# A two-stage attention and feed-forward kernel on one Trainium2 core: the fourth layer by seven products for every group of weights, with one planner for the whole second stage

## The chip, the cores and the metric

The kernel runs on one core of a Trainium2 chip, in one launch. The metric is the device time of that launch in microseconds (us). Its engines are named as the profile names them: PE is the matrix engine and PEld its weight loads, DVE the vector engine, ACT the scalar engine, POOL the GpSimd engine, SP the engine that issues the transfers.

## The reference

Attention over chunks of 64 tokens (4 batches, 8 heads, 576 tokens, 64 per head), then two feed-forward parts over 2304 tokens, all in float32:

```python
x = softmax(scale * q_c @ k_c.T) @ v_c        # per chunk of 64, then 2304 x 512
x = ((x @ w_a) * (x @ w_b)) @ w_out           # 512 -> 1536 -> 512
h = x @ w_in                                  # 512 -> 2048
g = np.maximum(h, 0.0) + alpha * np.minimum(h, 0.0)
out = g @ w2_out                              # 2048 -> 512
```

## The kernel before

**Numbers.** Every operand of a matmul is split in two: a high part, which ACT writes by a copy to the matmul's own type (*high*), and the rest, which DVE or POOL subtracts (*low*). A product is three matmuls: low by high, high by low, high by high. The weights arrive as 64-bit words and are turned into float32 on the way.

**Tokens.** The 2304 tokens are five blocks: block 0 has 256 of them, blocks 1 to 4 have 512 each.

**First stage** (up to 488 us). Attention, then the first feed-forward part: its 1536 inner columns are 12 chunks of 128 in six groups of two. For each group and block there are the products `pa` and `pb` and the sums `po` (lines 463 and 549). Beside this, in small steps (`job`, line 381), the second part's weights are converted, split, added up and written to DRAM (`w2_...`).

**Second stage.** The 2048 inner columns are eight groups of two chunks, and the token blocks 1 to 4 are two pairs. So there are 16 units q: group q with blocks 1 and 2 for q = 0 to 7, group q - 8 with blocks 3 and 4 for q = 8 to 15. Block 0 goes along with the first eight.

- *Third layer* (`seven`, line 644, and `third_layer`, line 913). Two chunks by two blocks by two halves of the depth are a 2 x 2 product, done by seven products in place of eight (`sumX`, `sumY`, `sumZ`), with sums of weights S1 to S4 and sums of tokens T1 to T4. ACT keeps what is in a PSUM bank (`c<-sumX`), DVE adds to it (`c<-sumY`, `c<-sumZ`), then come the two slopes (`g`), on DVE or on ACT with a last step on DVE. Block 0 has a plain product of 256 columns (`ph`, "small").
- *Fourth layer, plain* (`plain_layer`, line 1108): six matmuls of 512 columns for each 128 tokens (`po4`, which the profile's lists shorten to po) and one addition of 128x512 to the output's accumulator `oacc`. This is used for q = 0 to 5, and for block 0 always.
- *Fourth layer by seven products* (`half_layer`, line 1217): for two units d and d + 1 together (d = 6, 8, 10, 12, 14): seven products, each in two steps (hf) of twelve matmuls of 256 columns (`l4X`, `l4Y`, `l4Z`), each step with one addition of 128x2x256. It needs sums of g over the units (`g_sum`, line 1185: four for each unit) and seven splits in high and low for each unit in place of four (`g_halves_of`, line 1199), and sums of the w2_out weights, which `outer` (line 1295) loads, subtracts, splits and writes back to DRAM for each group.

**Order.** The first stage and unit q = 0 (lines 1723 to 1750) stand in an order written out by hand. From q = 1 on a `Planner` (line 56) sets it: each task has its engines with a cost, the tasks that it waits for, a due time and the buffers that it needs. It walks a clock of its own and emits the task that could begin first. The costs set nothing but this order; each engine then works its queue in it, waiting for semaphores. PE has two lists of fixed order, third and fourth layer, which `merge` (line 827) deals out in turn.

**Buffers.** Four PSUM banks are for the third layer, four for the fourth. The weights of a unit (`from_dram`, line 428) have buffers of their own per pool and tag, those of the fourth layer (`o_slots`, line 877) four sets in turn. The rest of the second stage draws 2 KB tiles from one stock (`slot`, `give`). The tokens' sums for the first pair come from `t_ops` (line 597), for the second pair from `token_sums` (line 1361): sums on DVE or POOL, highs on ACT, lows on POOL in `t_ops`, on either in `token_sums`.

Of the kernel before, what the change touches and what calls it, by code (L numbers as in the profile page):

```python
# [9 lines left out]
F32 = mybir.dt.float32  # L10
# [34 lines left out]
class Task:  # L45
    def __init__(self, kinds, f, deps, due, slots, rounded):
        self.kinds, self.f, self.due, self.slots, self.rounded = kinds, f, due, slots, rounded
        self.deps = [d for d in deps if d is not None]
        self.users = []
        self.left = len(self.deps)  # L50
        self.end = None
        for d in self.deps:
            d.users.append(self)


class Planner:
# [23 lines left out]
    def run(self):  # L80
# [12 lines left out]
        def begin(t, e):  # L93
            b = max([at[e]] + [d.end + self.HOP for d in t.deps])
# [15 lines left out]
        while count:  # L110
# [8 lines left out]
            for e, ts in lists.items():  # L119
                found = [(begin(t, e), t) for t in ts]  # L120
                found = [x for x in found if x[0] is not None]
                if e in ("DVE", "ACT", "POOL"):
                    kept = []
                    for b, t in found:
                        if len(t.kinds) > 1:
                            score = {}
                            for o in t.kinds:
# [3 lines left out]
                                score[o] = max(at[o], b if o == e else 0) + w + t.kinds[o][0] + t.kinds[o][2]  # L131
# [15 lines left out]
            at[e] = t.end - self.LAP[e] if e != "SP" else b + 0.06  # L147
# [22 lines left out]
def tile_attention_moe_moe2(ctx: ExitStack, tc: tile.TileContext, qkv, w_a, w_b, w_out, w2_in, alpha, w2_out, out):  # L170
# [14 lines left out]
    FIRST = 6  # L185
    RESERVE, NEAR, PEN, SLOPES = 6, 6.0, 0.6, 0.0
# [342 lines left out]

    def l2_mm(g, j, o):  # L530
# [63 lines left out]
    T = {}  # L594
    T_AT = {"B11": "xh1", "B21": "xl1", "T2": "xl2", "T1": "xh3", "T3": "xl3", "T4": "xh4", "B22": "xl4"}

    def t_ops(j1, j2, pause=()):
# [3 lines left out]
        t1, t2 = tt[:, 0:2], tt[:, 2:4]  # L601
        steps = []
# [41 lines left out]
    def seven(i, q, j1, j2, bare=None):  # L644
# [12 lines left out]
        wh, wl = W2[q, w]  # L657
# [73 lines left out]
    def rest_of_second_stage(G_all):  # L731
# [30 lines left out]
        for tag, own in (("a", 3), ("gh", 4), ("gl", 4)):  # L762
            for i in range(6):
                pool, n = (gp, own) if taken[tag] % 6 < own else (spares[0], 6 - own)
                taken[tag] += 1
                k = rings[pool, tag] = (rings[pool, tag] + 1) % n
                if tag == "a":
                    free0.append((0.5 + i / 4, (pool, f"{tag}{k}")))
                else:
                    held.append((i // 2, (pool, f"{tag}{k}")))  # L770
# [15 lines left out]
        DMA = {"SP": (2.8, False, 0)}  # L786
# [17 lines left out]
        for q in range(1, 2 * n2):  # L804
# [7 lines left out]
        def length(x):  # L812
            return {"seven": 6 * PER512, "small": 12 * PER256, "plain": 6 * PER512, "half": 12 * PER256}[x[0]]
# [50 lines left out]
        W_USERS = {0: (("seven", 0), ("seven", 1), ("small", 0)), 1: (("seven", 5), ("small", 1)), 4: (("seven", 2), ("seven", 3)), 5: (("seven", 4), ("seven", 6))}  # L864
        front_task = {}

        def add_front(q):
            for i, k, tag in ((0, 0, "a"), (1, 1, "a"), (4, 0, "b"), (5, 1, "b")):
                before = [pe_task.get((n, q - 2, x)) for n, x in W_USERS[i]]
                front_task[q, i] = plan.add(DMA, lambda t, i=i, k=k, tag=tag: from_dram(q, i, k, tag), before)  # L870

        osets = [(0.0, 2), (0.0, 3)]
        TW = {}
        o_prev = [None]
        o_task = {}

        def o_slots(kind):
            def f(t):
                where = osets.pop(0)[1]
                w = wps[where]  # L880
                both = []
                for n in range(2):
                    x = w.tile([P, 512], F32R, tag="o" + "hl"[n], name="tw")
                    if kind[0] == "plain":
                        _, q, k = kind
                        nc.sync.dma_start(out=x.bitcast(F32), in_=dram[2 * q % M2, 2 + k, n])
                    else:
                        _, d, p = kind
                        _, i, half = PRODUCTS[p]
                        for k in range(2):  # L890
# [3 lines left out]
                            )  # L894
                    both.append(x)
                TW[kind] = where, both
            return f

        o_users = []

        def add_o(kind, deps=()):

            before = o_users[-4] if len(o_users) >= 4 else []
            t = plan.add(DMA, o_slots(kind), list(deps) + [o_prev[0]] + before)
            o_prev[0] = o_task[kind] = t
            o_users.append([])
            return o_users[-1]

        def done_with(kind):
            osets.append((plan.now, TW.pop(kind)[0]))  # L910


        def third_layer(q):
# [4 lines left out]
            def product(i, deps):  # L918
# [5 lines left out]
                def f(t):  # L924
                    if opens:
                        st[name] = open_bank(t, "sum" + name, [P, 512]), t.place
                    seven(i, q, j1, j2, st[name][0])

                w = front_task.get((q, A_AT[a][0]))
# [116 lines left out]
        def small(q, k, st, slopes):  # L1046
# [3 lines left out]
            def f(t):  # L1050
                ph = open_bank(t, "ph", [P, 256])
                run(ph, k_steps(W2[q, k], xh[0], xl[0]))
# [3 lines left out]
            t = plan.add(pe(12 * PER256), f, [front_task.get((q, k))], due["small", q, k])  # L1056
# [51 lines left out]
        def plain_layer(q, j, t0):  # L1108
# [4 lines left out]
            def f(t):  # L1113
                po = open_bank(t, "po4", [P, DM])
                steps = []
                for k in range(2):
                    wh, wl = W2[q, 2 + k] if q == 0 else TW["plain", q, k][1]
                    if j == 0 and q > 0:
                        gh, gl = (x[:, 256 * k + t0 * P:256 * k + t0 * P + P] for x in GZ[q])
                    else:  # L1120
                        gh, gl = (x[:, t0 * P:t0 * P + P] for x in (GH[q, k, j] if q else first_G[q, k, j]))
# [3 lines left out]
                if t0 == blocks[j][1] - 1:  # L1125
                    if q == 0:
                        n = {1: 0, 2: 1, 0: 2}[j]
                        for i, where in held:
                            if i == n:
# [666 lines left out]
```

## Time and profile before

| | us |
|---|---|
| runs of the kernel, median of 3 (lowest, highest) | 871.47 (870.28, 871.96) |
| the profiled execution, whole | 870.09 |
| its span, first to last instruction | 868.1 |
| PE busy in the span | 851.5 (98%) |
| DVE, ACT, POOL busy | 585.7 (67%), 398.2 (46%), 411.7 (47%) |
| DMA, mean rate | 182 GB/s |

The span is that of one execution under the profiler; about 2 us of the device time lie around it. Busy times of PE are of overlapping matmuls, so its rate is read from the starts of successive groups, not from the time of one matmul. Times of day in the text ("488.0") are us from the span's start.

### The profile page before, as it was taken

Reading aid. Unit: us, or ns where it says so; the run is one execution under the profiler, and the core shown is the slowest. Engines: PE = TensorE matmul, PEld = TensorE weight load, DVE = VectorE, ACT = ScalarE, POOL = GpSimd, SP = SyncE. Lnnn points to the kernel's source line nnn. Section 1 sums busy time; section 2 is a strip of 40 time slices with the busy share of each in tenths; the row PEclk is TensorE's granted clock in tenths of the full one; section 3 lists DMA queues with packets and bytes.
Section 4 is the critical chain, followed back from the end, with each engine's and each line's share of the span. In section 5 each row is a group of like instructions: output and inputs, shape, how many; then the busy total and the mean of one; then the engine's idle time right before and its main releaser. Section 6 shows DMA issues by size and latency. Waiting matters only on the chain.

```text
span 868.1 us, 14796 instructions
## 1 busy us (share of the span) xinstructions
PE 851.5 (98%) x5520; PEld 731.3 (84%) x5520; DVE 585.7 (67%) x886; ACT 398.2 (46%) x709; POOL 411.7 (47%) x337
## 2 busy tenths in 40 slices
PE   7999999999999999999999989999999999999997
PEld 6788788888888888888888868888888899999997
DVE  6983446766766767677672784666658975677877
ACT  4673544544453444444451424443435554454441
POOL 4552335345545544563461787353424574532441
PEclk9999999999999999999999999999999999999999
DMA  8853115447536744763590255667653788566335
GB/s 314 294 177 108 24 60 164 163 132 251 188 100 216 257 135 146 251 202 126 190 319 24 74 195 208 206 217 263 223 169 99 244 268 275 191 204 205 119 97 170
DMA packets 106230, 157.74 MB, mean 182 GB/s; under 512 B 11952, under 2 KB 59056, under 8 KB 106160
## 3 DMA queue, kind: packets, MB, share of 16 engines
q1 hardware_dynamic: 106160, 156.81, 55.6%
q8 instruction: 43, 0.70, 0.3%
q14 instruction: 27, 0.22, 0.1%
HBM read 114.30 MB, written 42.47 MB: 181 GB/s over the span
## 4 chain that ended last, share of the span: by engine, by line
PE 48%; POOL 5%; DVE 5%; issue 4%; ACT 1%; POOLq 0%; DVEq 0%
PE po L463 13%; PE sumX L663 10%; PE l4X L1238 6%; PE sumZ L663 5%; PE l4Z L1238 3%; POOL t L261 3%; PE pa L463 3%; PE pb L463 3%; PE sumY L663 2%; PE ph L463 2%; POOL gl L486 2%; PE l4Y L1238 2%; DVE t L251 1%; DVE t L248 1%; DVE wl L271 1%
## 5 line engine op out<-in xcount | busy, mean ns | idle before, releaser
L486 POOL TENSOR_TENSOR gl<-a_sb,gh 128x512 fp32r<-128x512 f32 (+1 forms) x60 | 77.3, 1289 | 134.1 <-ACT gh L481 133.5
L261 POOL TENSOR_TENSOR t<-t,raw 128x512 int32<-128x512 int32 x68 | 90.3, 1328 | 104.1 <-DVE t L251 82.8
L463 PE MATMUL po<-gh,wl 128*128 128x512 f32 (+1 forms) x240 | 89.1, 371 | 1.0 <-DVE xl L1641 0.8
L463 PE MATMUL pb<-xh,wl 128*128 128x512 f32 (+1 forms) x240 | 88.9, 370 | 0.2 <-POOL wl L271 0.2
L463 PE MATMUL pa<-xh,wl 128*128 128x512 f32 (+1 forms) x240 | 89.0, 371 | 0.0
L463 PE MATMUL po<-gl,wh 128*128 128x512 f32 (+1 forms) x240 | 88.4, 368 | 0.0
L463 PE MATMUL pa<-xl,wh 128*128 128x512 f32 (+1 forms) x240 | 88.4, 368 | 0.0
L463 PE MATMUL po<-gh,wh 128*128 128x512 f32 (+1 forms) x240 | 88.3, 368 | 0.0
L463 PE MATMUL pa<-xh,wh 128*128 128x512 f32 (+1 forms) x240 | 88.3, 368 | 0.0
L463 PE MATMUL pb<-xh,wh 128*128 128x512 f32 (+1 forms) x240 | 88.3, 368 | 0.0
L463 PE MATMUL pb<-xl,wh 128*128 128x512 f32 (+1 forms) x240 | 88.3, 368 | 0.0
L663 PE MATMUL sumX<-T,w 128*128 128x512 f32 x288 | 74.0, 392 | 2.2 <-ACT c L939 2.2
L510 DVE TENSOR_TENSOR a_sb<-pb,a_sb 128x512 f32<-128x512 f32 (+1 forms) x60 | 37.9, 631 | 48.6 <-PE pb L463 42.3
L549 DVE TENSOR_TENSOR acc<-po,acc 128x512 f32<-128x512 f32 (+1 forms) x100 | 59.6, 628 | 8.0 <-PE po L463 8.0
L481 ACT ACTIVATE gh<-a_sb 128x512 fp32r<-128x512 f32 (+1 forms) x60 | 35.2, 586 | 64.1 <-DVE a_sb L510 63.9
L663 PEld LDWEIGHTS sumX<-T,w 128*128 128x128 f32 x288 | 52.4, 188 | 12.8 <-ACT c L939 3.1
L353 DVE TENSOR_TENSOR sl<-t,sh 128x512 fp32r<-128x512 f32 x32 | 24.7, 771 | 44.2 <-ACT sh L348 43.8
L251 DVE SCALAR_TENSOR_TENSOR t<-raw,t 128x512 uint32<-128x512 uint32 x68 | 52.1, 766 | 2.3
L463 PEld LDWEIGHTS po<-gh,wl 128*128 128x128 f32 x240 | 45.2, 188 | 9.5 <-DVE xl L1641 1.2
L463 PEld LDWEIGHTS pb<-xh,wl 128*128 128x128 f32 x240 | 45.2, 188 | 7.9 <-POOL wl L271 0.3
L463 PEld LDWEIGHTS pa<-xh,wh 128*128 128x128 f32 x240 | 45.2, 188 | 7.7
L463 PEld LDWEIGHTS po<-gh,wh 128*128 128x128 f32 x240 | 45.2, 188 | 7.6
(197 smaller groups left out, 2148.7 us busy)
## 6 DMA issues: line engine op xcount, KB each, us to landing
w<-w SPq DMA_DIRECT2D x148, 256.0 KB, 3.4
tw<-w SPq DMA_DIRECT2D x140, 128.0 KB, 2.8
raw<-in_moe_w_out SPq DMA_DIRECT2D x28, 512.0 KB, 3.7
w<-sh SPq DMA_DIRECT2D x48, 256.0 KB, 4.4
w<-sl SPq DMA_DIRECT2D x48, 256.0 KB, 4.5
qk_t<-in_qkv SPq DMA_DIRECT2D x18, 512.0 KB, 5.3
raw<-in_moe_w_in SPq DMA_DIRECT2D x16, 512.0 KB, 4.1
tw<-w SPq DMA_DIRECT2D x28, 256.0 KB, 4.9
```

Source lines behind the costliest of these rows:

```text
L248: nc.vector.tensor_scalar(out=t, in0=t, scalar1=3, scalar2=0x3FFFFFFF, op0=ALU.logical_shift_left, op1=ALU.bitwise_and)
L251: nc.vector.scalar_tensor_tensor(out=t, in0=raw[:, :, 1], scalar=0xC0000000, in1=t, op0=ALU.bitwise_and, op1=ALU.bitwise_or)
L261: nc.gpsimd.tensor_tensor(out=ti, in0=ti, in1=raw[:, :, 0].bitcast(I32), op=ALU.add)
L271: eng.tensor_tensor(out=wl, in0=wf, in1=wh.bitcast(F32), op=ALU.subtract)
L353: nc.vector.tensor_tensor(out=l, in0=wf, in1=h.bitcast(F32), op=ALU.subtract)
L463: nc.tensor.matmul(out=dst, lhsT=a, rhs=b, start=(i == 0), stop=(i == len(steps) - 1))
L481: nc.scalar.activation(out=h, in_=src, func=ACTF.Copy)
L486: nc.gpsimd.tensor_tensor(out=l, in0=src, in1=h.bitcast(F32), op=ALU.subtract)
L510: nc.vector.tensor_tensor(out=a_sb, in0=G[m, j], in1=a_sb, op=ALU.mult)
L549: nc.vector.tensor_tensor(out=acc[j][:, o, :], in0=po, in1=acc[j][:, o, :], op=ALU.add)
L663: nc.tensor.matmul(out=dst, lhsT=x, rhs=y, start=opens and kk == n == 0, stop=kk == 1 and n == 2, skip_group_check=not opens,)
L1238: nc.tensor.matmul(out=dst[:, tt], lhsT=x, rhs=y, start=opens and tt == i == 0, stop=i == 5, skip_group_check=tt > 0 or not opens,)
```

## The change

The fourth layer is done by seven products for all eight pairs of units (FIRST goes from 6 to 0). The planner now also orders unit q = 0, the last four steps of the first stage (`end_step`, block 4) and the tokens' sums of the first pair but for their first 14 steps. All weights of the second stage from unit 1 on are fetched into tiles of the common stock, which now has the buffers of the weight pools too (unit 0's come into the stock once they are used). A transfer or a weight sum is not begun earlier than a set time ahead of its due time. POOL is chosen only where it would finish first by the planner's clock, with the time counted at which it could begin. The last addition and its output transfer are cut in two.

```diff
-    FIRST = 6
-    RESERVE, NEAR, PEN, SLOPES = 6, 6.0, 0.6, 0.0
+    FIRST = 0
+    MORE, PACE = 8, 2
+    FAR1, FAR2, AHEAD = 140.0, 60.0, 5.0
+    RESERVE, NEAR, PEN, SLOPES = 4, 6.0, 0.6, 0.0
...
         def begin(t, e):
-            b = max([at[e]] + [d.end + self.HOP for d in t.deps])
+            b = max([at[e], t.due - t.early] + [d.end + self.HOP for d in t.deps])
...
-                                score[o] = max(at[o], b if o == e else 0) + w + t.kinds[o][0] + t.kinds[o][2]
+                                score[o] = max(at[o], b if o == e else begin(t, o)) + w + t.kinds[o][0] + t.kinds[o][2]
...
+        free0 += [(0.0, (wps[k], a + h)) for k in (2, 3) for a in "ab" for h in "hl"]
+        held += [(wps[k], "o" + h) for k in (2, 3) for h in "hl"]
...
-        DMA = {"SP": (2.8, False, 0)}
+        DMA = {"SP": (4.0, False, 2)}
+        DMA4 = {"SP": (4.5, False, 4)}
...
-        for q in range(1, 2 * n2):
+        for q in range(2 * n2):
             steps = [("seven", q, i) for i in range(7)]
...
-        merge(third[0][:1], [])
-        fourth += plain(0)
-        left = plain(0)
-        for q in range(1, FIRST):
-            nxt = third[q - 1][1 if q == 1 else 0:]
-            merge(nxt, left)
+        left = [("end", o) for o in range(KD)]
+        fourth += left
+        for q in range(FIRST):
+            merge(third[q], left)
             left = plain(q)
             fourth += left
         for d in range(FIRST, 2 * n2, 2):
-            merge(third[d - 1] + third[d], left)
+            merge(third[d] + third[d + 1], left)
             left = halves_steps(d)
             fourth += left
...
+        def use(kind):
+            readers[kind] -= 1
+            if readers[kind] == 0:
+                for x in WT.pop(kind):
+                    give(x)
...
+        def add_load(kind, deps=()):
+            t = plan.add(DMA4 if kind[0] == "half" else DMA, fetched(kind), deps, slots=2, rounded=True)
+            t.early = AHEAD
+            load_task[kind] = t
...
+        def end_step(o):
+            st = {}
+
+            def f(t):
+                st["po"] = open_bank(t, "po", [P, 512])
+                st["place"] = t.place
+                last_steps[o](st["po"])
...
+                if d == final and p == 6 and hf == 1:
+                    for i in range(2):
+                        nc.vector.tensor_tensor(out=a[:, i], in0=dst[:, i], in1=a[:, i], op=ALU.add)
+                        nc.sync.dma_start(out=out[r0 + i * P:r0 + i * P + P, cs], in_=a[:, i])
+                    return
...
-        def token_sums():
-            tt = {}
+        def token_sums(j1, j2, q0, begun):
+            tt = {"tt": begun} if begun is not None else {}
+            first = begun is not None
...
+        for q in range(2 * n2):
+            if q == 0:
+                token_sums(1, 2, 0, tt_of[0])
             if q == n2:
-                token_sums()
+                token_sums(3, 4, n2, None)
...
-                extra += [(f, ()) for f in early + steps]
+                extra += [(f, ()) for f in early + steps[:MORE]]
...
-        second[0] = True
-        for q in range(1):
-            j1, j2 = 1, 2
-            front = [(seven, (i, q, j1, j2)) for i in range(7)]
...
-        rest_of_second_stage(G)
+        second_stage({}, [lambda po, a=args: l2_into(po, *a) for _, args in behind])
```

In all, PE has 2496 matmuls of 512 columns where it had 2784, and 1968 of 256 columns where it had 1464; before 488 us its queue is the same. In DVE's queue there are 443 operations of two tensors of 128x512 (390 before), 69 of 128x256 (42) and 101 of 128x2x256 (68); in POOL's 183 of 128x512 (234) and 61 of 128x256 (86); in ACT's 644 of 128x512 (630). SP issues 704 transfers (619): 244 of 128x256 (158), the others nearly as many as before.

The first place is POOL's queue where the second stage begins. Before, with B and T the token sums' low parts (T2, T1, T3, T4, then B22):

```order
L618 TENSOR_TENSOR B_5244<-acc_1072,B_5244 128x512 x2
L618 TENSOR_TENSOR B_5265<-acc_1072,B_5265 128x512 x2
L618 TENSOR_TENSOR T_5301<-tt,T_5301 128x512 x2
L618 TENSOR_TENSOR T_5333<-tt,T_5333 128x512 x2
L618 TENSOR_TENSOR T_5358<-acc_1374,T_5358 128x512 x2
L618 TENSOR_TENSOR T_5378<-acc_1072,T_5378 128x512 x2
L486 TENSOR_TENSOR gl<-a,gh 128x512
L618 TENSOR_TENSOR B_5395<-acc_1374,B_5395 128x512 x2
```

And POOL's queue at the same place in the changed kernel:

```order
L632 TENSOR_TENSOR B_5244<-acc_1072,B_5244 128x512 x2
L632 TENSOR_TENSOR B_5265<-acc_1072,B_5265 128x512 x2
L1237 TENSOR_TENSOR l<-g,h 128x512
L1346 TENSOR_TENSOR ts<-w,ts 128x256
L1220 TENSOR_TENSOR S_5635<-g,S_5544 128x512
```

The ten low parts of T2, T1, T3, T4 and B22 have left POOL, and its next work after B11 and B21 belongs to the fourth layer.

The second place is DVE's queue there, in the changed kernel, from behind the last four additions of block 3 in the first stage. Before, it went from the sums `acc_1072<-acc_1072,tt` to `acc_1793<-po`, then to unit 0's `a<-sumY`:

```order
L1752 TENSOR_SCALAR minus_sb<-alpha_sb 128x16
L1416 TENSOR_TENSOR acc_1072<-acc_1072,tt 128x512 x2
L1433 TENSOR_TENSOR T_5297<-tt,T_5297 128x512 x2
L1433 TENSOR_TENSOR T_5303<-tt,T_5303 128x512
L1195 TENSOR_TENSOR acc_1793<-po,acc_1793 128x512
L1433 TENSOR_TENSOR T_5303<-tt,T_5303 128x512
L1433 TENSOR_TENSOR T_5317<-acc_1374,T_5317 128x512
L1433 TENSOR_TENSOR T_5331<-acc_1072,T_5331 128x512
L1433 TENSOR_TENSOR T_5317<-acc_1374,T_5317 128x512
L1346 TENSOR_TENSOR ts<-w 128x256
L1433 TENSOR_TENSOR T_5331<-acc_1072,T_5331 128x512
L1346 TENSOR_TENSOR ts<-w,ts 128x256
```

The ten low parts stand here now (T_5297 is T2, T_5303 T1, T_5317 T3, T_5331 T4, then B22), with the sums of weights for group 0 (`ts`) among them; unit 0's `c<-sumY` comes behind all of these.

The third place is DVE's queue near the end, where the last pair of units makes its sums S of g. Before:

```order
L1280 TENSOR_TENSOR oacc_8016<-l4Y,oacc_8016 128x2x256
L1208 TENSOR_TENSOR l<-S_9229,big 128x512
L1191 TENSOR_TENSOR S_9272<-g 128x512
L1280 TENSOR_TENSOR oacc_8016<-l4Y,oacc_8016 128x2x256
L1280 TENSOR_TENSOR oacc_7819<-l4X,oacc_7819 128x2x256
L1208 TENSOR_TENSOR l<-S_9272,h 128x512
```

And in the changed kernel:

```order
L1220 TENSOR_TENSOR S_9659<-g,S_9639 128x512
L1314 TENSOR_TENSOR oacc_8249<-l4Y,oacc_8249 128x2x256 x2
L1237 TENSOR_TENSOR big<-S_9659,h 128x512
L1237 TENSOR_TENSOR l<-S_9639,h 128x512
L1314 TENSOR_TENSOR oacc_8445<-l4Y,oacc_8445 128x2x256 x2
L1237 TENSOR_TENSOR l<-S_9724,h 128x512
```

The sum S1 (S_9272 before) is no longer in DVE's queue here, and the low part of S2 stands ahead of two of the additions.

## Rows read from the trace of the kernel before

**Rows 1.** The page's head: busy us, share of the span, instructions.

```profile
span 868.1 us, 14796 instructions
PE 851.5 (98%) x5520; PEld 731.3 (84%) x5520; DVE 585.7 (67%) x886; ACT 398.2 (46%) x709; POOL 411.7 (47%) x337
PEclk9999999999999999999999999999999999999999
```

**Rows 2.** Busy time by stretch, second stage; the columns are in its first line.

```profile
core 0: us, PE busy (x) PEld busy (x) DVE busy (x) ACT busy (x) POOL busy (x), PEclk, DMA share, GB/s
488.00:522.00 34.00, 31.04 (x145) 24.90 (x144) 26.26 (x29) 13.69 (x26) 30.32 (x23) 1.00 0.37 124
522.00:652.00 130.00, 130.00 (x634) 110.08 (x633) 81.22 (x125) 53.97 (x98) 58.89 (x58) 1.00 0.63 215
652.00:700.00 48.00, 47.88 (x253) 40.94 (x252) 41.12 (x59) 26.32 (x48) 25.07 (x18) 1.00 0.59 185
700.00:840.00 140.00, 140.00 (x903) 127.59 (x902) 99.16 (x137) 68.63 (x121) 60.88 (x44) 1.00 0.63 196
840.00:868.00 28.00, 23.33 (x186) 22.47 (x184) 21.45 (x29) 4.33 (x7) 9.95 (x7) 1.00 0.47 152
```

**Rows 3.** What PE waited for from 488 us on: us, times, longest.

```profile
PE sumX L663 <- ACT c L939: 2.2, 2, 1.5
PE sumZ L663 <- POOL B L618: 0.7, 1, 0.7
PE l4X L1238 <- DVE l L1208: 0.5, 1, 0.5
PE l4Z L1238 <- DVE l L1208: 0.4, 1, 0.4
```

**Rows 4.** The chain that ended last: start, us, piece; plain part, then seven products.

```profile
537.54 2.72 PE po L463 x12
...
563.58 2.72 PE po L463 x12
...
719.90 1.43 PE l4Z L1238 x12
...
759.38 1.43 PE l4Z L1238 x12
...
842.60 2.88 PE l4X L1238 x24
```

**Rows 5.** POOL's timeline where the second stage begins.

```profile
485.53 5.50 POOL L618 TENSOR_TENSOR B<-acc,B 128x512 fp32r<-128x512 f32 x4
490.99 6.14 POOL L618 TENSOR_TENSOR T<-tt,T 128x512 fp32r<-128x512 f32 x4
503.33 3.19 POOL L618 TENSOR_TENSOR B<-acc,B 128x512 fp32r<-128x512 f32 x2
```

**Rows 6.** DVE's timeline at the same place.

```profile
488.21 0.69 DVE L549 TENSOR_TENSOR acc<-po,acc 128x512 f32<-128x512 f32 x1 [0.67 <-PE po L463]
488.81 2.76 DVE L607 TENSOR_TENSOR acc<-acc,tt 128x512 f32<-128x512 f32 x2
495.89 1.27 DVE L549 TENSOR_TENSOR acc<-po,acc 128x512 f32<-128x512 f32 x2
```

**Rows 7.** DVE from 540 us on, by form: busy us, mean ns of one.

```profile
L944 DVE TENSOR_TENSOR c<-sumZ,c 128x512 f32<-128x512 f32 x28 | 19.3, 688 | 13.1 <-ACT c L939 10.3 <-PE sumZ L663 2.3
L1191 DVE TENSOR_TENSOR S<-g 128x512 f32<-128x512 f32 x2 | 2.4, 1222 | 0.0
L1313 DVE TENSOR_TENSOR ts<-w 128x256 f32<-128x256 f32 x2 | 0.8, 424 | 1.9 <-DMA w<-w 1.9
```

**Rows 8.** DMA issues: transfers, KB each, median us to landing.

```profile
w<-w SPq DMA_DIRECT2D x148, 256.0 KB, 3.4
tw<-w SPq DMA_DIRECT2D x140, 128.0 KB, 2.8
tw<-w SPq DMA_DIRECT2D x28, 256.0 KB, 4.9
```

**Rows 9.** Timelines of SP and DVE: one issue at 442 us, and the end.

```profile
442.19 0.38 SPq L356 DMA_DIRECT2D w<-sh  x1
...
864.25 0.69 DVE L1280 TENSOR_TENSOR oacc<-l4Z,oacc 128x512 f32<-128x512 f32 x1 [0.74 <-PE l4Z L1238]
...
860.65 4.69 SPq L1285 DMA_DIRECT2D out<-oacc  x6
```

More of the change, by code (lines that the diff above doesn't have):

```diff
@@ L528, in tile_attention_moe_moe2, with l2_into @@
     po_of = {}
+    def l2_into(po, g, j, o):
+        s = slice(o * P, (o + 1) * P)
+        steps = []
+        for m in groups1[g]:
+            wh, wl = WO[m]
+            gh, gl = G[m, j]
+            steps += [(wl[:, s], gh), (wh[:, s], gl), (wh[:, s], gh)]
+        run(po, steps)
     def l2_mm(g, j, o):
@@ L642, in sum_bank, with seven @@
         sums[name] = ring(pps[0], "p", 4, "sum" + name, F32, [P, 512])
-    def seven(i, q, j1, j2, bare=None):
+    def seven(i, q, j1, j2, bare=None, w_of=None):
         name, a, b = (
@@ L812, in length @@
         def length(x):
-            return {"seven": 6 * PER512, "small": 12 * PER256, "plain": 6 * PER512, "half": 12 * PER256}[x[0]]
+            return {"seven": 6 * PER512, "small": 12 * PER256, "plain": 6 * PER512, "end": 6 * PER512, "half": 12 * PER256}[x[0]]
         def plain(q):
@@ L861, in rest_of_second_stage, with fetched @@
         extra_slots = []
[L864 to L877, printed above, removed]
+        W_USERS = {
+            0: (("seven", 0), ("seven", 1), ("small", 0)), 1: (("seven", 5), ("small", 1)),
+            4: (("seven", 2), ("seven", 3)), 5: (("seven", 4), ("seven", 6)),
+        }
+        FRONT = {(n, x): i for i, users in W_USERS.items() for n, x in users}
+        WT = {}
+        readers = {}
+        load_task = {}
+        def use(kind):
[3 more added lines that the diff above has]
+                    give(x)
+        def fetched(kind):
             def f(t):
-                where = osets.pop(0)[1]
-                w = wps[where]
                 both = []
                 for n in range(2):
[L883 to L887, printed above, removed]
+                    x = slot("w", F32R)
+                    if kind[0] == "half":
                         _, d, p = kind
@@ L1164, in plain_layer, with add @@
             add_out((j, t0), [pe_task[key]], add, add, g == 0)
-            if j == 0 and t0 == 1:
-                for x in ("plain", q, 0), ("plain", q, 1):
-                    if x in o_list:
-                        o_list[x].append(pe_task[key])
+        def end_step(o):
[4 more added lines that the diff above has]
+                last_steps[o](st["po"])
+                if o == KD - 1:
+                    for where in held:
+                        plan.give(where)
+            pe_task["end", o] = plan.add(pe(6 * PER512), f, [], due["end", o])
+            pe_task["end", o].bank = 4
+            def add(t):
+                a = acc[4][:, o, :]
+                nc.vector.tensor_tensor(out=a, in0=st["po"], in1=a, op=ALU.add)
+                close_bank(4, st["place"])
+            add_out((4, "end", o), [pe_task["end", o]], add, add, False)
         started = set()
-        o_list = {}
         def source(q, n):
@@ L1245, in f @@
                             give(x)
[L1246 to L1248 removed]
+                use(("half", d, p))
+            sums_of = [outer_task[(d + k) % n2] for k in range(2)]
+            deps = [low_task[d, n], low_task[d + 1, n], need(("half", d, p), 1, sums_of)]
             if not opens:
@@ L1458, in fourth_until @@
                 rest4.pop(0)
-                for item in ring_items(x, None):
-                    if item not in o_list:
-                        deps = [] if item[0] == "plain" else [outer_task[(item[1] + k) % n2] for k in range(2)]
-                        o_list[item] = add_o(item, deps)
                 if x[0] == "plain":
```

190 lines of the change are left out of this document (80 added, 110 removed).

## The prediction

> **What bounds the kernel now.** I read the page's head first. PE is busy for 851.5 of 868.1 us, the other engines for 46 to 67%, and the granted clock is full in all 40 slices, the higher of its two levels, 2.4 GHz [rows 1]. By stretch [rows 2], PE has no gap from 522 to 652 and from 700 to 840 us, whichever form of the fourth layer runs; its gaps in the second stage lie in 488 to 522 (3.0 us) and 840 to 868. Who was waited for [rows 3]: 2.2 and 0.7 us at the start of the stage, on ACT's copy of a bank and on POOL's low part of B22; 0.5 and 0.4 us near the end, on two low parts from DVE. PE therefore works as a conveyor, and a change is worth what it takes off the belt, with what it does to these few waits. The rest is read from PE's chain [rows 4], from POOL's and DVE's timelines where the stage begins [rows 5, 6], from the cost of DVE's operations by form [rows 7], from the transfers [rows 8] and from the end [rows 9].
>
> The profiled execution took 870.09 us, 1.4 below the median of the three runs, 871.47. I sum against the execution and move the result up by that 1.4.
>
> **The change part by part.**
>
> *Columns.* Twelve matmuls of 512 columns take 2.72 us on the chain, 0.2267 each [rows 4]. Twelve of 256 take 1.43 and twenty-four 2.88 [rows 4], 0.1196 each within 0.0004. In the stretch with seven products, 14 products of the third layer (84 x 0.2267 = 19.04) and 14 steps of the fourth (168 x 0.1196 = 20.09) recur every 759.38 - 719.90 = 39.48 us [rows 4], which leaves 0.35 us for 14 changes from 256 to 512 columns, 0.025 each. The change removes 288 of the first kind (65.3 us) and adds 504 of the second (60.3 us); its order has 85 such changes where there were 68 (0.4 us). On the belt that is **-4.6 us**. Check by rows: a unit with the plain form takes 563.58 - 537.54 = 26.04 us [rows 4]; by the seven products two units take 39.48 and the four plain and four small steps of block 0, some 11.2, so 25.3 each, and six units give -4.1 even if every step alternates. Bounds: -4.1 to -5.2. In the Trainium skill, "TensorE: Matmul & The Clock Gate", section "Back-to-back issue gap" gives 518 cycles for 512 columns and 262 for 256 at 2.4 GHz; by these the sum would be 55.0 - 62.2 = -7.1 us, an estimate from the page. The rows are some 10 ns longer for either width, and they decide.
>
> *Start of the stage.* PE reaches it at 488.0 in both, since its queue is the same until there. Before, the ten low parts of T2, T1, T3, T4 and B22 were POOL's at 1.4 to 1.6 us each [rows 5], and B22's, which ran until 506.5, made PE wait. Now DVE does them. It is free at 488.9, and its two subtractions `acc<-acc,tt` take 2.76 us beside POOL [rows 6], which is done with B11 and B21 at 491.0 [rows 5] and then has nothing until the fourth layer. From 491.7 DVE needs about 0.64 us for each (1.27 for two [rows 6]). T2 is ready at 493.0, T1 (an addition in between) at 494.9, T3 at 496.8, T4 at 498 and B22 near 500. PE, with only one of the four end steps ahead of T3's product, wants the second half of T2 at 493.0, of T1 at 494.6, of T3 at 496.2. I count waits of 0.2, 0.4 and 0.6. Then the second small product of unit 0 needs a third-layer bank. Its bank is free when ACT has copied product 5 twice, behind the two copies of `c<-sumZ`, which DVE adds at about 501.1: near 503.5, where PE comes at 502.6, a wait of 0.9. That is 2.1 us in all against 2.9 [rows 3]: **-0.8 us**. Above it: everything lands 2 us later (+1.2). Below: none of it waits (-2.9).
>
> *DVE's load.* DVE gains 53 + 33 operations of 512 elements and 27 of 256; at 0.64 and 0.42 [rows 6, 7] that is 66 us, all in the second stage, where it was busy for 269 of 380 [rows 2]; POOL loses 76, so fewer of DVE's are drawn out. I take 330 of 374 us, 88%. What covers it is the slack on PE. By the order, the shortest way from a product through DVE back to PE in the steady part is still 4.1 us of matmuls, before and after, and such an eviction needs 0.7 to 1.4. Two stretches are fuller. Up to group 2's `c<-sumY` DVE has 61 operations, 34 us at those prices, for 33 us of matmuls; most of the stretch is the start just walked. While units 6 to 8 run, the token sums of the second pair fall in: 82 operations, 48 us, for 51.7 us of matmuls. An operation with both inputs in SBUF took 1222 ns where one that reads PSUM took 688 [rows 7], the former beside POOL. With some ten of POOL's in that stretch, DVE falls 2 us behind at most places and once perhaps more than the 4.1 of slack. I take **+1.0 us**; the ends are 0 (522 to 652 shows none, at 62% DVE) and +6.6 (below).
>
> *ACT* gains 14 operations of 512 and 8 of 2x256, 13 us at 0.6, at 46% load [rows 1]: nothing, since it is never waited for after the start. If it were, its copy of `sumX` has 1.4 us of matmuls, as before.
>
> *Loads.* SP issues 85 more transfers. PE waits for no transfer in the stage [rows 3]. By the order, the shortest lead between the last event that a load's queue waits for and its use is 7.2 us of matmuls; before it was 6.1, and that one was in time. Landing takes 2.8 to 4.9 [rows 8]: nothing. Its other end is a rival.
>
> *End of the stage.* The waits of 0.5 and 0.4 us [rows 3] were for low parts of S2 and S1, which had 1.8 us of matmuls for a chain of three of DVE's operations. S1 is on POOL now and the shortest way is 3.3 us: **-0.9 us**, at worst 0. The last addition (0.69 [rows 9]) becomes two of 256 with a transfer each: the first leaves 0.3 us earlier, the second as late as before with half the bytes; SP needs 0.78 per issue here (4.69 for six [rows 9]). Nothing, within 0.4 either way. *The score rule, AHEAD, FAR and RESERVE* set only the order, which is what I counted.
>
> **Sum.** -4.6 - 0.8 + 1.0 - 0.9 = -5.3. The profiled execution would be 864.8, the median **866.2 us**.
>
> **The rivals.**
>
> 1. *DVE is full while units 6 to 8 run.* For it: 48 of 51.7 us without any drawing out. If 27 of the 82 meet POOL and take 0.54 longer each (1.222 - 0.688 [rows 7]), DVE needs 62.5, is 10.8 late, and PE, with 4.2 of slack, waits 6.6 where I took 1.0: 866.2 + 5.6 = 871.8, no change. Against it: POOL has half its work left. Chance 0.13.
> 2. *Weights come late* (the slower side). The place is SP's queue, in the 28 weight sets of the seven-product steps before unit 8, four transfers each where a plain set had two. The shortest lead is 7.2 us; four issues at 0.38 [rows 9] leave 5.6. If a landing under load takes 6.1, a set is late by 0.5 and the sum is 28 x 0.5 = 14 us: 880. It ends slower once landings pass 5.9 (28 x 0.25 = 7). Against it: 4.9 is the longest median in its rows [rows 8], the load per us grows by a few per cent, and most leads are over 9 us. Chance 0.07.
> 3. *The start is worse.* The 29 operations of 488 to 522 took 26.3 us [rows 2], some 8 more than their bare prices, because POOL was busy for 30.3. If DVE, now with 34 us of work there, is drawn out as much, it is 9 us late; with the whole of it on PE the gain turns into 874. Against it: POOL has left that stretch. Chance 0.04.
> 4. *All waits go.* None at the start, none from DVE: -4.6 - 2.9 - 0.9 = -8.4, so 863.1. Chance 0.12.
> 5. *A narrow matmul costs just half of a wide one.* By rows 504 x 0.1133 = 57.1, so -8.2 for the columns and 862.6. The skill's page just named would have it nearly so, and this case's 1.43 us for twelve [rows 4] speaks against it. Chance 0.02.
>
> That the change does not do what it says is excluded: the matmuls of either width were counted in its queue.
>
> **How the numbers follow.** My forecast has 0.62, with a range of its own of 863.8 to 869 from the bounds above. With rivals 1 (0.13), 2 (0.07), 3 (0.04), 4 (0.12) and 5 (0.02), the range of 8 in 10 is 863.0 to 871.6: it leaves out 2, 3 and 5 and parts of 1 and 4. A measurement of this kernel can tell 0.2%, 1.7 us, from no change. Faster by more than that, below 869.7: the forecast and rivals 4 and 5, 0.76. Within: rival 1, 0.13. Slower, above 873.2: rivals 2 and 3, 0.11.
>
> **What would show it.** Right: the piece of two units before 652 us repeats every 50 to 51 us in place of 52.1; PE's waits name DVE's low parts (`T<-tt,T`) and ACT's `r<-sumX` near 493 to 504 and sum to 2 us; none near the end; DVE near 88% of the stage and POOL's share down by a third. Wrong: a wait of PE on a transfer of `w` (rival 2); waits on `c<-sumZ` or on closings between 640 and 700 (rival 1); over 5 us of gaps before 530 (rival 3). A pitch other than 0.12 us in the new steps would break the first term.

## The result, and the profile after

The changed kernel took **861.98 us** (median of four runs, 861.24 to 864.14), the kernel before 870.88 beside it: a ratio of 0.9903, interval 0.9879 to 0.9926. That is 8.9 us faster where 5.3 were forecast, and 1.0 us below the low end of the range.

The head of the changed kernel's page, then its busy time by stretch, with the columns of [rows 2]:

```profile
span 862.0 us, 15567 instructions
PE 849.5 (99%) x5736; PEld 741.1 (86%) x5736; DVE 628.7 (73%) x997; ACT 412.9 (48%) x731; POOL 319.1 (37%) x261
```

```profile
488.00:522.00 34.00, 33.59 (x168) 27.51 (x167) 31.73 (x54) 20.42 (x38) 10.03 (x9) 1.00 0.39 132
522.00:652.00 130.00, 130.00 (x822) 118.08 (x821) 113.04 (x185) 69.47 (x126) 43.39 (x35) 1.00 0.84 273
652.00:700.00 48.00, 48.00 (x305) 43.56 (x304) 44.49 (x68) 27.04 (x49) 16.39 (x12) 1.00 0.70 231
700.00:840.00 140.00, 140.00 (x905) 127.66 (x905) 109.68 (x166) 63.14 (x109) 22.66 (x17) 1.00 0.70 219
840.00:868.00 28.00, 18.24 (x151) 17.86 (x149) 14.46 (x22) 2.45 (x4) 3.21 (x3) 0.93 0.28 95
```

Against [rows 1, 2]: POOL's work in the stage has halved (185 to 96 us), DVE is at 93% from 652 to 700 and at 85% over the stage (313.4 us), and PE has no gap between 522 and 840. The list of what PE waited for from 488 us on, to be held against [rows 3]:

```profile
PE l4Y L1267 <- issue: 0.3, 1, 0.3
PE ph L466 <- ACT r L988: 0.2, 1, 0.2
```

This trace is of the slowest of the four runs (864.14), and what made it so lies ahead of the change: its first product of the second stage (`sumX`) starts at 490.84 us, in the kernel before at 488.01. Matmul for matmul, this trace falls behind that of e9 (the same kernel once more, below) by 2.5 us up to 48 us, and by hardly anything after that. In the windows of its first 40 us the granted clock, the number behind POOL's count, falls below 1.00, where before had 1.00 in each:

```profile
8.00:16.00 8.00, 6.46 (x176) 5.61 (x168) 7.75 (x16) 3.23 (x7) 4.85 (x4) 1.00 1.04 376
16.00:24.00 8.00, 6.60 (x151) 5.86 (x149) 6.64 (x14) 6.21 (x11) 4.31 (x4) 0.79 0.72 228
24.00:32.00 8.00, 5.05 (x134) 4.35 (x136) 5.85 (x10) 3.00 (x6) 4.43 (x3) 0.95 0.85 293
32.00:40.00 8.00, 8.00 (x187) 7.39 (x180) 7.16 (x10) 5.39 (x10) 3.71 (x4) 0.84 0.90 312
```

The clock alone does not set the delay: of two experiments told below, e7's trace has the same mean over its first 40 us as this one, 0.91, and reaches the stage at 489.02; e6's has 0.96 and reaches it at 490.98. What else delays the first 40 us stays open.

So from here on I compare the **stage**: from the start of the first `sumX` to the start of the last but one `l4Z` matmul. Before it is 863.81 - 488.01 = 375.80 us, now 858.14 - 490.84 = **367.30**, 8.50 shorter. From there to the end of the span it is 4.29 before and 3.86 now. Together that is the 8.9.

Of each stage I also give what PE **lost**: by PE's timeline, start to start, every group of matmuls (six wide, twelve narrow, or several of them in a row) that took over 0.06 us longer than its kind does undisturbed ([rows 4]; a wide group ahead of a narrow one with the 0.025 of a change), and by how much, summed. Before it is 6.05 us: 4.07 up to 522 us, 0.48 at 684, 1.50 from 845 on. Now it is 1.97: 1.43 up to 506 us and 0.54 at an `l4Y` near 842. What is left is matmuls alone, the **rest**: 375.80 - 6.05 = 369.75 before, 367.30 - 1.97 = 365.33 now. So the columns gave 4.4 and the losses 4.1.

The forecast's pitch holds. In the chain of the changed kernel the same step of each pair of units recurs every 50.60 us, where two plain units took 52.1:

```profile
543.63 1.44 PE l4Y L1267 x12
...
594.23 1.44 PE l4Y L1267 x12
...
644.83 1.44 PE l4Y L1267 x12
```

### The profile page after: what moved, and what is told of

Its sections match the earlier page's. It is cut to its first block, busy times and chain, and to the rows that moved or that the text cites. A ratio compares the mean times of both kernels' runs of the same rounds, so it can differ in the third digit from the quotient of the medians.

```text
span 862.0 us, 15567 instructions
## 1 busy us (share of the span) xinstructions
PE 849.5 (99%) x5736; PEld 741.1 (86%) x5736; DVE 628.7 (73%) x997; ACT 412.9 (48%) x731; POOL 319.1 (37%) x261
## 4 chain that ended last, share of the span: by engine, by line
PE 88%; DVE 4%; POOL 3%; issue 2%; DMA 1%; ACT 1%; SPq 1%; DVEq 0%; POOLq 0%
PE po L466 17%; PE pa L466 15%; PE pb L466 15%; PE l4X L1267 10%; PE sumX L677 10%; PE l4Z L1267 5%; PE sumZ L677 5%; PE l4Y L1267 3%; PE ph L466 3%; PE sumY L677 2%; POOL t L264 1%; POOL gl L489 1%; PE s L1647 1%; PE pt L1625 1%; PE s L1589 1%
## 5 line engine op out<-in xcount | busy, mean ns | idle before, releaser
L1267 PE MATMUL l4X<-w,h 128*128 128x256 f32 x364 | 71.4, 283 | 0.0
L677 PE MATMUL sumX<-T,w 128*128 128x512 f32 x254 | 67.6, 393 | 0.1
L561 DVE TENSOR_TENSOR acc<-po,acc 128x512 f32<-128x512 f32 (+1 forms) x96 | 57.0, 626 | 5.9 <-PE po L466 5.9
L1267 PEld LDWEIGHTS l4X<-w,h 128*128 128x128 f32 x364 | 57.5, 191 | 1.2
L356 DVE TENSOR_TENSOR sl<-t,sh 128x512 fp32r<-128x512 f32 x32 | 24.7, 770 | 44.0 <-ACT sh L351 43.6
L961 ACT ACTIVATE c<-sumX 128x512 f32<-128x512 f32 x48 | 28.6, 597 | 54.7 <-PE sumX L677 47.6
L254 DVE SCALAR_TENSOR_TENSOR t<-raw,t 128x512 uint32<-128x512 uint32 x68 | 52.1, 766 | 2.3
L677 PEld LDWEIGHTS sumX<-T,w 128*128 128x128 f32 x254 | 45.7, 189 | 8.8 <-DVE T L1433 0.9
```

The source lines that it names most:

```text
L254: nc.vector.scalar_tensor_tensor(out=t, in0=raw[:, :, 1], scalar=0xC0000000, in1=t, op0=ALU.bitwise_and, op1=ALU.bitwise_or)
L356: nc.vector.tensor_tensor(out=l, in0=wf, in1=h.bitcast(F32), op=ALU.subtract)
L561: nc.vector.tensor_tensor(out=acc[j][:, o, :], in0=po, in1=acc[j][:, o, :], op=ALU.add)
L677: nc.tensor.matmul(out=dst, lhsT=x, rhs=y, start=opens and kk == n == 0, stop=kk == 1 and n == 2, skip_group_check=not opens,)
L961: nc.scalar.activation(out=st[n], in_=st["X"][0], func=ACTF.Copy)
L1267: nc.tensor.matmul(out=dst[:, tt], lhsT=x, rhs=y, start=opens and tt == i == 0, stop=i == 5, skip_group_check=tt > 0 or not opens,)
```

## The experiments

Each was timed in five rounds beside the kernel before, in three sets (e1 to e4, e5 to e8, e9 to e12), where before had 871.04, 869.30 and 869.89 us.

| | us | ratio to before, interval | stage | lost | rest |
|---|---|---|---|---|---|
| before | 870.88 |  | 375.80 | 6.05 | 369.75 |
| changed | 861.98 | 0.9903 (0.9879 to 0.9926) | 367.30 | 1.97 | 365.33 |
| e1 new order, six plain units | 864.68 | 0.9929 (0.9909 to 0.9948) | 370.47 | 0.73 | 369.74 |
| e2 two plain units | 863.96 | 0.9920 (0.9903 to 0.9937) | 369.03 | 2.26 | 366.77 |
| e3 low parts on POOL again | 863.81 | 0.9918 (0.9902 to 0.9935) | 369.16 | 3.83 | 365.33 |
| e4 last addition whole | 862.56 | 0.9902 (0.9884 to 0.9920) | 367.31 | 1.99 | 365.32 |
| e5 end steps in unit 0 | 861.14 | 0.9902 (0.9889 to 0.9915) | 366.25 | 0.88 | 365.37 |
| e6 and runs of two | 860.40 | 0.9896 (0.9883 to 0.9909) | 365.53 | 0.79 | 364.74 |
| e7 changed, all sums on DVE | 861.20 | 0.9908 (0.9896 to 0.9921) | 366.81 | 1.50 | 365.31 |
| e8 loads without limit | 888.28 | 1.0213 (1.0191 to 1.0235) | 392.03 | 26.90 | 365.13 |
| e9 changed again | 862.09 | 0.9905 (0.9890 to 0.9919) | 367.22 | 1.90 | 365.32 |
| e10 e6 with all sums on DVE | 859.27 | 0.9883 (0.9865 to 0.9902) | 365.15 | 0.46 | 364.69 |
| e11 loads 20 us ahead | 865.49 | 0.9946 (0.9932 to 0.9961) | 371.27 | 5.94 | 365.33 |
| e12 before, low parts on DVE | 869.15 | 0.9988 (0.9977 to 0.9999) | 374.67 | 4.92 | 369.75 |

The stage repeats better than the time: e9 is the changed kernel once more, 367.22 beside 367.30, and e4 has 367.31. The rest repeats to 0.1 us among kernels with the same matmuls in much the same order; e8's is 0.2 below, with 73 changes from 256 to 512 columns in place of 85.

**e1, the order without the columns.**

```diff
-    FIRST = 0
+    FIRST = 6
```

> The new order, stock and engines, but the plain fourth layer for the first six units, as before: PE has the old 2784 matmuls of 512 columns and 1464 of 256. My theory, as it stands after the result, splits the 8.9 us into 4.6 for the columns and 4.3 for the start, the end and the tail: so 866.6 us, 0.995 of before, with the second stage from the first sumX to the last l4Z some 4.5 us longer than in the changed kernel, all of it between 522 and 652 us. Rival A, that seven products carry the whole gain: 870.9 and no difference from before. Rival B, that narrow matmuls cost just half of wide ones (8.2 for the columns): 870.2.

Measured 864.68, two us better than expected. The order and the engines alone, with before's matmuls, shorten the stage by 5.33 us, all of it losses (6.05 to 0.73). From e1 to the changed kernel the columns give 4.4 (369.74 to 365.33) and 1.2 is lost again at the start. Both rivals fall. In the Trainium skill, "TensorE: Matmul & The Clock Gate", section "Back-to-back issue gap", the gaps for the two widths would have made the columns worth 7.1 us (an estimate from that page); the traces say 4.4.

**e2, one pair of units back.**

```diff
-    FIRST = 0
+    FIRST = 2
```

> The changed kernel with the plain fourth layer for units 0 and 1 alone, a third of e1's step back. If the columns' price holds (4.6 us for six units), one pair of units is worth 1.5: 863.5 us. If DVE's load in units 0 and 1, at the start, cost PE something that I do not see (rival), the time is 862 or less.

Measured 863.96. The rest is 366.77 against 365.33: 1.4 us for the pair, a third of 4.4, as expected. Its losses are near the changed kernel's in size, but they lie in one group at the start (1.7 us), where PE waits for DVE's low part of a T.

**e3, the first pair's low parts back on POOL.**

```diff
-lows.append(plan.add(LESS, low, [hs[kk]] + lows[:1]))
+lows.append(plan.add({"POOL": (1.3, True, 0)} if first else LESS, low, [hs[kk]] + lows[:1]))
```

> The changed kernel, but the low parts of the first pair's token sums are POOL's alone again, as before the change. My theory is that DVE's taking them over is what the start gained (2.5 us where I predicted 0.8): PE waits again for POOL's B22 and for copies, 2 to 3 us by the list of waits, and the second stage is 2 to 2.5 us longer, 864.3. The rival is that the start gained through the planner's order of unit 0, whichever engine writes the low parts: within 0.5 of 862.0.

The stage is 1.86 us longer, a little less than I gave, and the rival falls. The theory holds in part: PE waits for POOL and for a copy again, 2.0 us by the list, but for low parts of T; B22's is not named:

```profile
PE sumX L677 <- POOL T L1433: 1.4, 3, 0.7
PE sumX L677 <- ACT c L961: 0.6, 1, 0.6
```

**e12, the inverse: that one thing in the kernel before.**

```diff
-            nc.gpsimd.tensor_tensor(out=t[:, 1, kk], in0=src[:, kk], in1=t[:, 0, kk].bitcast(F32), op=ALU.subtract)
+            e = nc.gpsimd if name in ("B11", "B21") else nc.vector
+            e.tensor_tensor(out=t[:, 1, kk], in0=src[:, kk], in1=t[:, 0, kk].bitcast(F32), op=ALU.subtract)
```

> The kernel before with one thing of the change alone: the ten low parts of T2, T1, T3, T4 and B22 at the start of the second stage are DVE's, in the same hand-written order. e3, the inverse in the changed kernel, cost 1.7 us of stage. If the engine alone makes the start, the old stage of 375.8 becomes 374.1 or shorter, 869.5 beside 871. The rival is that the old written order puts these low parts ahead of evictions in DVE's queue, so that the waits only change their name: 375.5 to 377.

The stage is 1.13 us shorter: less than the 1.7 expected, and not the rival's case either. The wait for B22 is gone, those for ACT's copies are as before [rows 3]:

```profile
PE sumX L664 <- ACT c L940: 2.3, 2, 1.4
```

So of 2.6 us that the start gained, the engine alone gives 1.1 in the old order, and the rest needs the planner's order; taken out of the new order, the engine is worth 1.9 (e3).

**e4, the end.**

```diff
-                if d == final and p == 6 and hf == 1:
-                    for i in range(2):
...
-                    return
```

> The changed kernel with the last addition and its transfer whole, as before. From the last matmul to the end of the span took 4.29 us before and 3.86 in the changed kernel, where I had predicted no difference. If the cut made that, this stretch is 4.2 to 4.4 us again and the time 862.4; if it varies from run to run by as much, it is anywhere from 3.8 to 4.4. The verdict is the stretch in the trace, since the time cannot tell 0.4 us.

From the end of the stage to the end of the span: 4.14 us with the addition whole here, 4.3 in both traces of the old order (before and e12). With the cut it is 3.9 in eight of eleven traces (changed, e3, e6 to e11, with e9 as the changed kernel once more), but 4.2 to 4.4 in the other three (e1, e2, e5). A saving of 0.2 to 0.4 us is likely; since three traces lack it and what sets them apart is not known, it is not shown.

**e5 and e6, the start mended, then fewer changes of width.**

```diff
-            merge(third[d] + third[d + 1], left)
+            if d == 0:
+                merge(third[0], left)
+                merge(third[1], [])
+            else:
+                merge(third[d] + third[d + 1], left)
```

> The changed kernel with its four end steps of the first stage dealt out among the steps of unit 0 alone, not of units 0 and 1 together; each first unit's product but one then has one of them behind it, as in e1. Its second stage lasted 367.3 us, with four groups at the start that took 1.55 to 1.8 us in place of 1.36 (1.4 us over in all), while the list of waits names 0.2; e1, with its end steps in unit 0, was 0.2 over there. If the thin spread is what the products wait on, the stage is 366.1 and the time 860.8. The rival is that DVE is simply short at the start: then unit 1, without any fourth-layer work, waits in its place, and the time is 862 or more.

e6 adds to this that `merge` takes two steps at a time from a list, from unit 2 on:

```diff
-        def merge(a, b):
+        def merge(a, b, n=2):
...
-                x = a.pop(0) if a and (not b or len(a) / na >= len(b) / nb) else b.pop(0)
-                due[x] = clock
-                clock += length(x)
+                x = a if a and (not b or len(a) / na >= len(b) / nb) else b
+                for _ in range(n):
+                    if x:
+                        y = x.pop(0)
+                        due[y] = clock
+                        clock += length(y)
```

> e5 with third- and fourth-layer steps dealt out in runs of two from unit 2 on, so that PE's queue changes from 256 to 512 columns 55 times in place of 85. A group of six wide matmuls takes 1.39 us before a narrow one and 1.36 before a wide one. If each change of width costs these 0.03 us, the stage is 0.9 shorter than in e5. The rival is that two third-layer products in a row leave their banks' evictions less cover: then waits on closings or copies appear and take back more than 0.9.

e5's stage is 366.25, 1.05 shorter, as expected; the times' intervals do not part it from the changed kernel. In e5 the start loses 0.35 where the changed kernel loses 1.43. e6's stage is another 0.72 shorter, where 0.9 was expected: 0.63 of it in the rest, by 30 changes of width (0.021 each), with one group over by 0.40 that e5 did not have.

**e7 and e10, DVE's load.**

```diff
-        LESS = {"DVE": (0.692, True, 0), "POOL": (1.3, True, PEN)}
-        LESS256 = {"DVE": (0.42, True, 0), "POOL": (0.74, True, PEN)}
+        LESS = {"DVE": (0.692, True, 0)}
+        LESS256 = {"DVE": (0.42, True, 0)}
```

> The changed kernel with every addition, subtraction and low part for which the planner could choose, 56 of 128x512 and 13 of 128x256 that are POOL's in it, on DVE. By 0.64 and 0.42 us each this is 41 us more for DVE, which was busy for 313 of the stage's 367 us: some 96%. The prediction gave DVE's load 1.0 us at 88% and the changed kernel showed none at 85%. If load itself reaches PE once it is near full, PE waits on DVE's operations for 3 to 8 us in all, most of it between 652 and 700 us, where DVE was already at 93%: 865 to 870. The rival: PE's queue leaves every eviction enough slack as long as DVE is not over 100%, and DVE's operations get shorter when POOL is quiet: within 1 us of 862.

My own expectation fell: the stage is 366.81, and less is lost than in the changed kernel. The windows of e7:

```profile
522.00:652.00 130.00, 130.00 (x825) 118.21 (x824) 117.24 (x209) 66.04 (x121) 0.00 (x0) 1.00 0.81 263
652.00:700.00 48.00, 48.00 (x306) 43.62 (x306) 45.97 (x79) 28.09 (x52) 0.00 (x0) 1.00 0.74 247
700.00:840.00 140.00, 140.00 (x908) 127.81 (x907) 119.51 (x191) 64.86 (x112) 0.00 (x0) 1.00 0.68 215
```

DVE took 69 more operations, 41 us by their bare price, and is busy for only 15.7 more in the stage (313.4 to 329.1). The rest came back from its other operations. The sums S of g by form, from 488 us on (busy us, mean ns of one), in the changed kernel and in e7:

```profile
L1220 DVE TENSOR_TENSOR S<-g,S 128x512 f32<-128x512 f32 x26 | 21.4, 825 | 0.4
L1220 DVE TENSOR_TENSOR S<-g 128x512 f32<-128x512 f32 x23 | 16.9, 734 | 0.4
```

```profile
L1220 DVE TENSOR_TENSOR S<-g 128x512 f32<-128x512 f32 x32 | 21.9, 686 | 0.9 <-PE sumZ L677 0.7
L1220 DVE TENSOR_TENSOR S<-g,S 128x512 f32<-128x512 f32 x32 | 21.5, 686 | 0.3
```

These means mix two kinds of operation. Set beside POOL's operations by their times of day, 39 of the changed kernel's 49 sums S run while POOL does nothing, and take 676 to 694 ns each. The other ten meet an operation of POOL: four still take 0.68 to 0.69 us, six take 1.22 to 1.67. The 1222 ns of [rows 7] is the mean of only two, 679 without POOL and 1765 beside it. In e7, without POOL, all 64 take 679 to 695, which is what one that reads PSUM takes throughout. e10 puts both together, the two edits shown for e6 and e7:

> e6 with all the stage's additions and low parts on DVE, as in e7. e6 had a stage of 365.4 us, e7 of 366.9 where the changed kernel had 367.3. If DVE's load is free up to there even with two third-layer products in a row, and DVE's operations are only shorter for POOL's silence, the stage is 365.0 to 365.4. The rival is that runs of two leave a full DVE too little slack: waits on closings return and the stage is over 366.5.

Its stage is 365.15 and no wait of PE is listed in it. At 859.27 us it is the fastest of all, 2.8 below the changed kernel on the same chip:

```profile
span 857.4 us, 15475 instructions
PE 844.6 (99%) x5736; PEld 737.9 (86%) x5736; DVE 646.8 (75%) x1071; ACT 407.4 (48%) x721; POOL 228.8 (27%) x192
```

**e8 and e11, the loads.** Both change how far ahead of its due time a transfer may begin. First e11's edit, then e8's, which drops the limit:

```diff
-    FAR1, FAR2, AHEAD = 140.0, 60.0, 5.0
+    FAR1, FAR2, AHEAD = 140.0, 60.0, 20.0
```

```diff
-            t.early = AHEAD
+            t.early = 1e9
```

> The changed kernel without the limit by which a weight's transfer begins at most 5 us ahead of its due time. The prediction counted the loads as nothing: the shortest lead was 7.2 us, the median landing 3 to 5. If they are in time already, earlier ones change nothing: within 0.5 us of 862. If a few are late in a way that the waits do not name, the stage gets shorter by up to 1 us. Against that, early loads hold tiles of the stock that others then wait for: up to 2 us longer.

> The changed kernel with loads allowed 20 us ahead of their due time in place of 5 (e8, without any limit, was 26 us longer, with PE waiting 11.4 us for transfers by name). My theory of e8 is that loads far ahead hold tiles of the stock, so that a load which is due soon finds none and stands late in SP's queue. At 20 us ahead some four times as many tiles are held as at 5: part of the loss, 2 to 10 us over 862, with PE waiting on transfers. The rival is that any load out of due order spoils SP's queue, so that 20 does as much harm as no limit, 885; or that harm begins only far out, within 1 us of 862.

e8 missed by far: 26 us slower than the changed kernel, 24.7 in the stage. Its list of PE's waits, and SP's timeline where the longest one falls:

```profile
PE l4X L1267 <- DMA w<-w: 10.9, 4, 7.5
PE sumX L677 <- ACT r L988: 2.7, 1, 2.7
PE l4Y L1267 <- DVE l L1237: 1.8, 1, 1.8
PE sumY L677 <- DVE B L1433: 1.4, 1, 1.4
```

```profile
693.06 1.85 SPq L903 DMA_DIRECT2D big<-w  x4
694.96 0.90 SPq L908 DMA_DIRECT2D big<-w  x2
696.05 2.62 SPq L903 DMA_DIRECT2D w<-w  x4
...
702.26 9.80 SPq L903 DMA_DIRECT2D w<-w  x10
```

PE stood on an `l4X` from 697 to 704.5 while SP issued one load after another. The waits named in e8 come to 18.2 us and its losses to 26.9; some of the difference is the clock. Behind that stand the two next `l4X` steps took 3.13 and 2.29 us in place of 1.43, and the granted clock from 690 to 715 us was 0.80 on average, between its two levels, where the changed kernel's is 1.00 from 488 to 840.

e11, at 20 us, loses 4.0 us of stage, as expected, but with only 0.5 us on a transfer by name; its other named waits are for ACT's copies and one addition of DVE's. That fits a stock short of tiles, which would delay every task that needs one; how many tiles were held at which time I did not measure, so this part of the mechanism is argued, not shown. What is shown: in this kernel earlier loads cost time, and the limit is one of the parts of the change that carry it.

Left open: the old stock and order with seven products for the first six units, and the new order with the old rule for choosing POOL, were not tried.

## Why the prediction was wrong

| term | predicted | measured | from |
|---|---|---|---|
| columns | -4.6 | -4.4 | the rest; e1, e2 |
| start of the stage | -0.8 | -2.6 | groups that ran over |
| DVE's load | +1.0 | 0 | no wait from 522 to 840; e7 |
| end of the stage | -0.9 | -1.0 | groups that ran over |
| a `po` at 684 us | not in the sum | -0.5 | a group that ran over |
| tail | 0, within 0.4 | -0.4 | likely the cut; e4 |

**Columns: right**, in size and in mechanism. **Loads and ACT: right** as nothing; the limit that keeps the loads so was passed over in a sentence as part of "the order", and e8 shows what rival 2 looks like without it.

**The start: the step that failed most, on both of its sides.** For before I took the 2.9 us of the list of waits [rows 3] as what the waits cost. They cost 4.07. Here is PE's timeline of before around the two waits for ACT's copies; a group of six wide matmuls takes 1.36:

```profile
512.15 0.61 PE L463 MATMUL po<-w,gh 128*128 128x512 f32 x2
513.54 1.65 PE L663 MATMUL sumX<-T,w 128*128 128x512 f32 x6 [0.78 <-ACT c L939]
515.03 0.39 PE L463 MATMUL po<-w,gl 128*128 128x512 f32 x1
...
517.75 0.39 PE L463 MATMUL po<-w,gl 128*128 128x512 f32 x1
...
520.72 1.66 PE L663 MATMUL sumX<-T,w 128*128 128x512 f32 x6 [1.45 <-ACT c L939]
522.22 0.39 PE L463 MATMUL po<-w,gl 128*128 128x512 f32 x1
```

The step `po` begins at 517.75 and would be done by 519.11; `sumX` starts at 520.72, 1.61 later, of which the list names 1.45, and takes 520.72 to 522.22 = 1.50 in place of 1.36. The wait named 1.45 cost 1.75, the one named 0.78 cost 1.07, and B22's, named 0.73, cost 1.03, since its group took 2.39 us. A `sumZ` that took 1.58 adds 0.22 with no entry at all.

Part of the gap between list and cost is how the list counts. A matmul of 512 columns stands in the trace for 0.39 us while the next can start 0.2267 after it, and the list counts idle time from the end of that 0.39: 0.16 of every wait, and the whole of a shorter one, has no entry. (At B22's wait two matmuls start 1.12 apart; less 0.39, that is the 0.73 named.)

For the changed kernel I walked four waits of 2.1 us together. Its timeline there:

```profile
490.84 1.52 PE L677 MATMUL sumX<-B,w 128*128 128x512 f32 x6
...
493.56 1.52 PE L677 MATMUL sumY<-B,w 128*128 128x512 f32 x6
494.92 1.74 PE L677 MATMUL sumX<-T,w 128*128 128x512 f32 x6
496.50 1.87 PE L677 MATMUL sumZ<-T,w 128*128 128x512 f32 x6
498.21 1.96 PE L677 MATMUL sumX<-T,w 128*128 128x512 f32 x6
500.01 0.40 PE L466 MATMUL po<-gh,wl 128*128 128x512 f32 x1
```

The three products with T2, T1 and T3 take 1.58, 1.71 and 1.80, over by 0.22, 0.35 and 0.44; the one for the bank, behind a `po` at 504.2, costs 0.42 where I had 0.9. That is 1.43 in all, and the list names 0.2 of it. What these groups met shows in DVE's low parts beside the fourth matmuls of the products with T1 and T3:

```profile
496.90 0.68 DVE L1433 TENSOR_TENSOR T<-tt,T 128x512 fp32r<-128x512 f32 x1
497.63 0.73 PE L677 MATMUL sumZ<-T,w 128*128 128x512 f32 x2
```

```profile
497.50 1.88 DVE L1433 TENSOR_TENSOR T<-acc,T 128x512 fp32r<-128x512 f32 x3
499.44 0.73 PE L677 MATMUL sumX<-T,w 128*128 128x512 f32 x2
```

T1's second low part ends at 497.58 and the matmul starts at 497.63; T3's, the third of its row, ends at 499.38 and the matmul starts at 499.44. The places were right, and the first three grew in the order forecast; the fourth, forecast as the largest, was not. The sum was 0.7 too high. 4.07 - 1.43 = 2.6 in place of 0.8.

**DVE's load: the second step that failed.** I drew its operations out as beside before's POOL, with 1222 ns, a mean of two (679 and 1765), as the price of one, and let that reach PE. But the change that loads DVE is the one that quiets POOL, and with it the drawing out goes (e7). 85% of the stage and 93% in the fullest part cost PE nothing between 522 and 840 us, and in e7, at 90%, PE lost less than in the changed kernel. Rival 1 stood on the same mistake.

**The end**: the forecast removed the two named waits, 0.9, and left none. The size came out, by two errors that cancel. By groups these waits cost 0.79 and 0.61, with 0.1 beside, 1.50 in all: the same error as at the start. And the changed kernel has a new loss of 0.54, at an `l4Y` near 842 us, which the list puts at "issue". A sum S that DVE makes just there takes 1.52 us, beside POOL; without POOL, in e7, the same place loses 0.09. That it was this sum which PE waited for is likely and not shown. Apart from the end, before lost 0.48 at a `po` at 684 us, with no entry in the list; the changed kernel does not, and the forecast had no term for it.

Two rivals came near the measured -8.9 by luck. Rival 5 gave -8.9 itself, by columns worth 8.2, and the columns gave 4.4. Rival 4, "all waits go", gave -8.4, but some waits stayed, and those that went were worth more than their names.

## What to carry to other kernels

Price a wait of a saturated engine by the pitch of its groups, start to start, against the pitch where nothing waits; the list of waits left out 0.3 us of each here, and most of the short ones. Where work moves from POOL to DVE, take away the stretch that POOL put on DVE's other operations before judging the load: 69 operations worth 41 us cost 16. And a load that is in time gains nothing from being earlier: without the limit of 5 us this kernel lost some 25 us.

## What was not expected of the hardware

- A named wait of PE cost about 0.3 us more than its entry. About half of it lies ahead of the group that waited, where the list does not count, and half within it (1.50 in place of 1.36 us): the first matmul behind a wait was followed by the next after 0.34 us in place of 0.23. A group whose operands came just after it could have used them was 0.2 to 0.45 us longer with no entry.
- DVE's sums of two inputs in SBUF took 0.68 to 0.69 us whenever POOL did nothing, and mostly 1.2 to 1.8 us where they met one of its operations (in before and in the changed kernel); those that read PSUM stayed at 680 to 690 ns on average either way. With POOL silent they kept to 0.69 although ACT was busy for half of the time and the transfers went on (e7).
- The granted clock of the first 40 us differs from execution to execution (0.91 on average in the changed kernel's trace, between the two levels, 1.00 in that of e9), and the start of the second stage moves by up to 3 us, though not by the clock alone. That is a third of the whole gain, and the reason to compare stages.
